# Two attention blocks on one core: a third score bank on loan by default, products with V gathered longer, and GpSimd held while VectorE makes a shift

## The chip, the core and the metric

The kernel runs on one core of a Trainium2 chip. The core has five engines that run their own queues in order and meet through semaphores: TensorE (PE, with PEld for its weight loads), VectorE (DVE), ScalarE (ACT), GpSimd (POOL) and SyncE (SP), which here only issues DMA transfers. The metric is the device time of one execution in microseconds, as the median of some runs; lower is better.

## The reference: what is computed

Two independent blocks with 2048 tokens, width 512 and 32 heads of 16 columns. Their outputs lie side by side in one 2048 x 1024 result. Block A is linear attention, block B is full softmax attention:

```
def _A_ref(x, wqkv, wo):      # q, k, v from x @ wqkv, 32 heads of 16
    phi = lambda t: jnp.where(t > 0, t + 1, jnp.exp(t)) + 1e-6
    pq, pk = phi(q), phi(k)
    kv = jnp.einsum("bhsd,bhse->bhde", pk, v)
    z = jnp.einsum("bhsd->bhd", pk)
    num = jnp.einsum("bhqd,bhde->bhqe", pq, kv)
    den = jnp.einsum("bhqd,bhd->bhq", pq, z)[..., None] + 1e-6
    o = num / den             # heads joined, @ wo
def _B_ref(x, wqkv, wo):
    scores = jnp.einsum("bhqd,bhkd->bhqk", q, k) * Dh ** -0.5
    p = _softmax(scores, axis=-1)
    o = jnp.einsum("bhqk,bhkd->bhqd", p, v)   # heads joined, @ wo
```

Nearly all the work is block B: 32 heads x 2048 x 2048 scores, each of which needs an exponential.

## The kernel before, in words

The scores are cut into 32 units (a group of eight heads, 512 query columns, one of two halves of the heads), and each unit into 64 blocks of 128 keys x 512 queries: 2048 blocks. A block's score product is one matmul from 32 rows of QT and KM into one PSUM bank (L863). Its exponential is made in one of two ways.

- **The exact way.** ScalarE takes the exponential of two or three neighbouring banks of pS in one instruction (L1095) and writes PT. There are two such slots, one of three banks and one of two (ABL), used in turn. A block then needs one product with V (L1224).
- **The approximate way**, called D here. VectorE turns one bank of scores into 16-bit integers whose bits are a half-precision number close to the exponential (L970, into DI, two banks at once where they lie side by side). Two shifted copies of it are needed as well (L1166, into DJ); a group of three blocks (DG) is shifted by one instruction of 1536 columns, twice. GpSimd makes most of these shifts, VectorE a few. A D block needs three products with V, one with each of DI and the two DJ, against three scaled copies of V (L671 makes the two scaled ones).

PSUM has eight banks: five for the slots, one for the sum of products with V (pPV), two for everything else (pD): D blocks, the projections of both blocks, block A. The third bank of the wide slot can be *lent* to that other work; the slot is then filled with two blocks instead of three (fill_act_cand, want_lend). Block A and the projections are jobs of a few stages each (Job) which the program threads between the blocks.

The order on every engine is not written by hand. A planner in the kernel's own Python code keeps a clock for each engine and a price for each operation, picks again and again the operation that can start first, and records it (Sched.add). From the recorded order it puts a semaphore wait wherever one engine reads or overwrites what another made. The engines then run their recorded queues in order. Constants near the top set the planner's habits: LD, LB and PB5 when the third bank is lent, VHI how many finished blocks may wait before products with V are preferred, PBL how much shift work may pile up, LATE how close to ScalarE's need a slot is filled, JU when a job may start ahead of its due time, SEEDS a random scatter of those due times by stages of 45 us.

In shift_cand (L1148) a shift goes to VectorE where GpSimd's pile is over LM = 5 us longer; its planned price there is 0.40 + w * 0.0003 us.

## Time and profile before

| what | us |
|---|---|
| median of 3 runs | 683.81 (683.69 to 686.09) |
| the profiled execution: its time | 684.12 |
| the profiled execution: span from first to last instruction | 682.4 |
| ScalarE busy | 669.0 (98%) |
| PE busy (matmul) | 653.9 (96%) |
| GpSimd busy | 622.1 (91%) |
| VectorE busy | 582.6 (85%) |
| granted TensorE clock, mean | 0.997 |

Busy time of an engine is the union of its instructions. Neighbouring instructions on ScalarE and VectorE overlap a little in the record, so the time that one more instruction costs is the distance between two starts, not the duration of one; both are used below. A PE that is busy in the record is not a PE at its peak.

### The profile page before, as it was taken

The numbers are of one execution on the slowest core, as the hardware profiler recorded it, in microseconds if no ns is written. First come the engines' busy times: TensorE is split into PE (matmuls) and PEld (weight loads), VectorE is DVE, ScalarE is ACT, GpSimd is POOL, SyncE is SP. The second block draws the span as 40 slices with busy tenths as digits, with TensorE's granted clock in tenths as the row PEclk, the third lists the DMA queues.
The fourth block names the chain that finished last, engine by engine and source line by source line (L and its number), as shares of the span: only waits on it lengthen the run. The fifth ranks groups of instructions, "written<-read, shape, count | busy, mean of one in ns | idle before, by whom it ended". The sixth has DMA issues, their size and how long they took to land.

```text
span 682.4 us, 19594 instructions
## 1 busy us (share of the span) xinstructions
PE 653.9 (96%) x8530; PEld 209.9 (31%) x8530; DVE 582.6 (85%) x937; ACT 669.0 (98%) x706; POOL 622.1 (91%) x470
## 2 busy tenths in 40 slices
PE   8999999999999999999999999999999999999997
PEld 4323333222323333332322233222332222322223
DVE  5878898999789988868999898888888998898983
ACT  5999999999999999999999999999999999999997
POOL 6698999999699999999999999999999999999894
PEclk9999999999999999999999998999999999999999
DMA  9400012011101201130111000111010110001111
GB/s 207 103 2 2 17 16 35 10 31 23 34 2 33 33 17 17 22 82 11 24 25 33 24 18 18 24 47 25 18 36 13 33 32 25 9 17 33 47 41 35
DMA packets 55418, 21.76 MB, mean 32 GB/s; under 512 B 45600, under 2 KB 55328, under 8 KB 55328
## 3 DMA queue, kind: packets, MB, share of 16 engines
q1 hardware_dynamic: 54128, 20.07, 13.4%
q8 instruction: 68, 1.11, 0.7%
q10 hardware_dynamic: 1200, 0.39, 0.2%
q14 instruction: 22, 0.18, 0.1%
HBM read 4.19 MB, written 4.19 MB: 12 GB/s over the span
## 4 chain that ended last, share of the span: by engine, by line
ACT 87%; POOL 7%; PE 3%; DVE 2%; DMA 1%; issue 0%; ACTq 0%
ACT PT L1095 85%; POOL DJ L1166 6%; ACT pD L683 1%; DVE DI L970 1%; PE pS L863 1%; DMA xTb<-in_B_x_dram 1%; ACT pS L683 1%; PE pD L535 1%; PE pPV L1224 1%; PE pS L535 1%; PE pS L654 0%; POOL XN L1359 0%; ACT KV L539 0%; POOL VV L671 0%; DVE DJ L1166 0%
## 5 line engine op out<-in xcount | busy, mean ns | idle before, releaser
L1095 ACT ACTIVATE PT<-pS 128x1024 f16<-128x1024 f32 (+1 forms) x666 | 660.5, 1353 | 2.6 <-PE pS L863 1.8
L1166 POOL TENSOR_SCALAR DJ<-DI 128x1536 int16<-128x1536 int16 (+1 forms) x391 | 579.5, 1483 | 48.0 <-DVE DI L970 21.6
L970 DVE TENSOR_SCALAR DI<-pD 128x512 uint16<-128x512 f32 (+1 forms) x456 | 315.2, 705 | 48.4 <-PE pD L863 42.8
L863 PE MATMUL pS<-QT,KM 32*128 32x512 bf16 x1573 | 261.5, 385 | 21.3 <-ACT PT L1095 15.0
L1224 PE MATMUL pPV<-PT,VV 128*17 128x512 f16 (+1 forms) x1420 | 244.0, 378 | 0.5 <-DVE OT L1354 0.5
L1224 PE MATMUL pPV<-DJ,VV 128*17 128x512 f16 (+1 forms) x1256 | 231.9, 379 | 0.7 <-POOL DJ L1166 0.5
L863 PE MATMUL pD<-QT,KM 32*128 32x512 bf16 x475 | 168.5, 385 | 0.3 <-DVE PQT L684 0.3
L863 PEld LDWEIGHTS pS<-QT,KM 32*128 32x128 bf16 x1573 | 64.3, 91 | 278.0 <-ACT PT L1095 260.3
L1224 PE MATMUL pPV<-DI,VV 128*17 128x512 f16 (+1 forms) x628 | 148.3, 379 | 0.5 <-DVE OT L1354 0.4
L970 DVE TENSOR_SCALAR DI<-pS 128x512 uint16<-128x512 f32 x153 | 104.1, 681 | 8.0 <-PE pS L863 4.4
L1224 PEld LDWEIGHTS pPV<-PT,VV 128*17 128x17 bf16 x1420 | 49.8, 88 | 44.0 <-issue 38.1
L1224 PEld LDWEIGHTS pPV<-DJ,VV 128*17 128x17 bf16 x1256 | 47.9, 88 | 47.2 <-issue 35.6
L863 PEld LDWEIGHTS pD<-QT,KM 32*128 32x128 bf16 x475 | 39.7, 91 | 9.3 <-issue 4.1
L1224 PEld LDWEIGHTS pPV<-DI,VV 128*17 128x17 bf16 x628 | 31.2, 88 | 22.4 <-issue 18.4
L1166 DVE TENSOR_SCALAR DJ<-DI 128x1536 int16<-128x1536 int16 x29 | 28.3, 977 | 0.0
L535 PE MATMUL pD<-xTb,Wb 128*32 128x512 bf16 (+1 forms) x368 | 26.7, 379 | 0.0
L535 PE MATMUL pD<-Wa,xTa 128*32 128x256 bf16 x672 | 26.4, 275 | 0.0
L1354 DVE STREAM_TRANSPOSE OT<-pPV 128x512 f32<-128x512 f32 x31 | 22.0, 708 | 0.7 <-PE pPV L1224 0.6
L1359 POOL TENSOR_TENSOR XN<-OT,ZRA 128x256 bf16<-128x256 f32 x31 | 19.5, 630 | 1.2
L683 ACT ACTIVATE pD<-pD 128x512 f32<-128x512 f32 x22 | 19.6, 893 | 0.0
L671 POOL TENSOR_SCALAR VV<-VV 128x544 bf16<-128x544 bf16 x24 | 17.3, 723 | 0.9
L535 PEld LDWEIGHTS pD<-Wa,xTa 128*32 128x32 bf16 x672 | 15.4, 96 | 8.7 <-issue 5.4
(109 smaller groups left out, 392.3 us busy)
## 6 DMA issues: line engine op xcount, KB each, us to landing
out_dram<-KV SPq DMA_DIRECT2D x31, 128.0 KB, 1.7
Wa<-in_A_wqkv_dram SPq DMA_DIRECT2D x3, 512.0 KB, 4.2
KM<-KR SPq DMA_DIRECT2D x96, 16.0 KB, 1.8
Wb<-in_B_wqkv_dram SPq DMA_DIRECT2D x2, 384.0 KB, 4.6
Wb<-in_B_wqkv_dram SPq DMA_DIRECT2D x1, 512.0 KB, 4.4
Wa<-in_A_wo_dram SPq DMA_DIRECT2D x1, 512.0 KB, 4.5
Wb<-in_B_wo_dram SPq DMA_DIRECT2D x1, 512.0 KB, 3.8
xTa<-in_A_x_dram SPq DMA_TRANSPOSE x24, 3.4
```

The lines of the kernel that those rows point to most:

```text
L535: ins = e.matmul(out[32 * g:32 * g + 32], lhsT=lhsT[:, 32 * g:32 * g + 32], rhs=rhs, start=start, stop=stop, tile_position=(0, 32 * g))
L671: st.append((lane, 0.74 if lane == "dve" else VVT, f_op(lane, lambda e, k=k: e.tensor_scalar(vv(k), vv(0), SW[k], 0.0, op0=ALU.mult, op1=A ...
L683: ex = lambda bk: sch.add("act", lambda e: e.activation(x(bk), x(bk), ACTF.Exp), reads=[bk[3]], writes=[bk[3]])
L863: return e.matmul(dst, lhsT=KM[32 * g:32 * g + 32, Gp % 2, e_, j * 128:(j + 1) * 128], rhs=QT[32 * g:32 * g + 32, Gp % 2, c * 512:(c + 1) ...
L970: sch.add("dve", lambda e: e.tensor_scalar(DI.bitcast(U16)[:, buf, i * 512:(i + n) * 512], f32v(DBANK[bi], 512 * n), EB, IMAX, op0=ALU.add ...
L1095: sch.add("act", lambda e: e.activation(PT[:, row, c0:c0 + w], SCR[sl][:, 0:w], ACTF.Exp, scale=SC / ESC), reads=skeys(sl)[:len(bl)], writ ...
L1166: sch.add(ln, lambda e: e.tensor_scalar(J, I, 1.0, float(SH[k]), op0=ALU.mult, op1=ALU.add), reads=[("DI", buf, i) for i in range(n)], wri ...
L1224: sch.add("pe", lambda e: e.matmul(dst[32 * g:32 * g + 17, 0:n], lhsT=VV[:, Gp % 2, k, j, 17 * h:17 * h + 17], rhs=P[:, q0:q0 + n], start= ...
L1354: sch.add("dve", lambda e: e.transpose(OT[:, 0, :], PVb[:, 0:512]), reads=[("PV", g) for g in range(4)], writes=[("OT", 0)])
L1359: mul = f_op("pool" if XNP else "dve", lambda e: e.tensor_tensor(xn[:, :, 16 * e_:16 * e_ + 16], o[:, :, 0:16], zr.unsqueeze(2).broadcast_ ...
```

## The change

What it does, part by part:

- **Lending.** want_lend now lends the third bank whenever no bank of pD is free at that time and VectorE's and GpSimd's piles are under LB = 2 and PB5 = 9 us (LD = 2), or when more banks are held by jobs than are lent. Before, it was lent while a job held a bank or waited for one.
- **Gathering.** The threshold VHI (24), and with it DLEAD, JU, LATE and PBL, become five sets, MODES; each stage of 45 us takes the set that its seed selects. The thresholds in the sets are 28, 36 or 48.
- **Holding.** When VectorE makes a shift, or a scaled copy of V, the next instruction recorded for GpSimd gets a wait for it (Sched.hold). The planner's price of such a shift on VectorE becomes 0.45 us after the end of GpSimd's running instruction.
- **The first products** (first_units) use the whole width of the array instead of four tiles of 32 columns, and the planner's starting clocks change, GpSimd's from 16.0 to 8.4.
- DG stays 3. SEEDS is new, so jobs are due at other times.

The core of the diff ("..." marks what is left out):

```
+        self.hold = []
...
+        if lane == "pool" and self.hold:
+            extra_deps = list(extra_deps) + self.hold
+            self.hold = []
...
-    PVW = 0.3
+    PVW = 0.0
-    LD = 1
-    LB = 99.0
-    PB5 = 3.0
+    LD = 2
+    LB = 2.0
+    PB5 = 9.0
-    PBL = 7.5
-    SEEDS = (0, 195, 365, 131, 7, 89, 76, 286, 0, 222, 34, 197, 397, 382, 371)
+    SEEDS = (0, 242, 225, 232, 372, 115, 142, 52, 152, 183, 352, 31, 0, 263, 361)
-    VHI = 24
+    MODES = ((0.8, 36, 0.7, 0.2, 9.0), (1.2, 36, 0.7, 0.2, 9.0), (0.8, 48, 0.9, 0.2, 10.5), (1.2, 28, 0.7, 0.1, 9.0), (1.0, 36, 0.55, 0.35, 8.0))
+    LDA = 1
+    JM = 0.8
+    DSH = 0.45
...
+        def mode():
+            return MODES[SEEDS[min(int(T["pe"] / SEG), len(SEEDS) - 1)] % len(MODES)]
...
-                        ins = mm4(e, bk[0][:, bk[2] + o0:bk[2] + o0 + n], Wb[:, cc, kind * 512:kind * 512 + 128], xTb[:, cc, c0:c0 + n], cc == 0, cc == 3)
+                        ins = e.matmul(bk[0][:, bk[2]:bk[2] + n], lhsT=Wb[:, cc, kind * 512:kind * 512 + 128], rhs=xTb[:, cc, c0:c0 + n], start=(cc == 0), stop=(cc == 3))
...
+                if lane == "dve":
+                    def alone(bk, cp=cp):
+                        sch.hold.append(cp(bk))
+                        sch.hold[-1].x = 0.27
+                    alone.kind = "x"
+                    st.append(("dve", 0.27, alone))
...
         def want_lend(t_):
...
+            free = sum(1 for x in dfree if x is not None and x <= t_ + 0.1)
+            if LD == 2 and sum(1 for i in range(len(dfree)) if held.get(i)) > sum(lent):
+                return True
+            if free:
                 return False
...
+            return d_backlog(t_) <= LB and p_backlog(t_) <= PB5
...
-            dp, dd = POOLT(w), 0.40 + w * 0.0003
+            dp, dd = POOLT(w), DSH + max(0.0, T["pool"] - sd)
...
+                if ln == "dve":
+                    T["pool"] = max(T["pool"], vis("dve", en_))
...
+                if ln == "dve":
+                    sch.hold.append(op)
+                    op.x = DSH
...
-            pr = 1 if out_ >= VHI or final else 4
+            pr = 1 if out_ >= mode()[1] or final else 4
...
-        T.update(pe=7.75, act=7.4, dve=9.05, pool=16.0)
+        T.update(pe=7.8, act=7.4, dve=9.2, pool=8.4)
```

Where the instructions stand now. Line numbers of the changed kernel are larger (L1095 becomes L1111, L1166 becomes L1184, L970 becomes L988, L535 becomes L544 and, for the first products, L573, L863 becomes L881, L654 becomes L664).

ScalarE, from its first exponential on; 1024 columns are two banks, 1536 are three. Before:

```order
L1095 ACTIVATE PT<-pS 128x1024 x14
L1095 ACTIVATE PT<-pS 128x1536
L1095 ACTIVATE PT<-pS 128x1024
L1095 ACTIVATE PT<-pS 128x1536
L1095 ACTIVATE PT<-pS 128x1024
L1095 ACTIVATE PT<-pS 128x1536
L1095 ACTIVATE PT<-pS 128x1024
L1095 ACTIVATE PT<-pS 128x1536
```

And in the change:

```order
L1111 ACTIVATE PT<-pS 128x1024 x6
L1111 ACTIVATE PT<-pS 128x1536
L1111 ACTIVATE PT<-pS 128x1024 x13
L1111 ACTIVATE PT<-pS 128x1536
L1111 ACTIVATE PT<-pS 128x1024 x3
L1111 ACTIVATE PT<-pS 128x1536
L1111 ACTIVATE PT<-pS 128x1024 x15
L1111 ACTIVATE PT<-pS 128x1536
```

Three-bank exponentials come one at a time between long rows of two-bank ones; over the program they go from 86 to 65 and the two-bank ones from 579 to 604.

PE, its first products after the warm-up; before:

```order
L535 MATMUL pS<-xTb,Wb 32x128 x16
L535 MATMUL pD<-xTb,Wb 32x256 x32
L535 MATMUL pS<-xTb,Wb 32x384 x16
L863 MATMUL pS<-QT,KM 128x512 x2
L535 MATMUL pD<-xTb,Wb 32x512 x16
L863 MATMUL pS<-QT,KM 128x512 x5
```

And in the change:

```order
L573 MATMUL pS<-xTb,Wb 128x128 x4
L573 MATMUL pD<-xTb,Wb 128x256 x8
L573 MATMUL pS<-xTb,Wb 128x384 x4
L544 MATMUL pD<-xTb,Wb 32x512 x8
L881 MATMUL pS<-QT,KM 128x512 x2
L881 MATMUL pD<-QT,KM 128x512
```

The 64 narrow products become 16 wide ones, and half of the next projection (8 tiles of L544) now stands ahead of the first scores.

VectorE, near the end of the program: the last rows of the last unit but one, up to the transpose (L1354, then L1374) that closes it. Before:

```order
L539 CAST KV<-pD 128x512
L970 TENSOR_SCALAR DI<-pD 128x512 x2
L970 TENSOR_SCALAR DI<-pS 128x512
L970 TENSOR_SCALAR DI<-pD 128x512 x2
L970 TENSOR_SCALAR DI<-pS 128x512
L539 CAST KV<-pD 128x512
L970 TENSOR_SCALAR DI<-pD 128x512
L1354 STREAM_TRANSPOSE OT<-pPV 128x512
```

And in the change:

```order
L988 TENSOR_SCALAR DI<-pD 128x512
L1184 TENSOR_SCALAR DJ<-DI 128x1536
L548 CAST KV<-pD 128x512
L1184 TENSOR_SCALAR DJ<-DI 128x1536
L548 CAST KV<-pD 128x512
L988 TENSOR_SCALAR DI<-pD 128x512
L988 TENSOR_SCALAR DI<-pS 128x512
L988 TENSOR_SCALAR DI<-pD 128x512 x2
L1374 STREAM_TRANSPOSE OT<-pPV 128x512
```

Shifts (DJ<-DI) now stand in VectorE's queue between the evictions; there are 64 of them in the program instead of 29, and GpSimd has 364 of three blocks instead of 389.

More of the change, by code (lines that the diff above doesn't have):

```diff
@@ L19 @@
     __slots__ = ("idx", "lane", "fn", "pos", "waits", "sig", "count", "vc",
-                 "name", "queue")
+                 "name", "queue", "x")
 class Sched:
@@ L53, in add @@
         op.sig = force_signal
+        op.x = None
         op.count = 0
@@ L1049, in fill_act_cand @@
             start = max(T["pe"], t0, afree[sl], ptfree.get((row, sl), 0.0) - 0.5)
-            if sl == 0 and wd == ABL[0] and lent[0]:
-                start = max(start, dfree[ND])
+            if sl in LIX and wd == 3 and lent[sl]:
+                start = max(start, dfree[LIX[sl]])
             dur = switch("q") + 0.22
-            late = T["act"] + sum(exps) - dur - TAIL["pe"] - SEM - LATE
+            late = T["act"] + sum(exps) - dur - TAIL["pe"] - SEM - mode()[3]
             if nfill[0] >= NS and start < late:
@@ L1061, in run @@
                 nfill[0] += 1
-                if sl == 0 and wd == ABL[0]:
-                    dfree[ND] = None
-                    lent[0] = False
-                elif sl == 0 and not lent[0]:
-                    dfree[ND] = st
-                    lent[0] = True
+                if sl in LIX and wd == 3:
+                    dfree[LIX[sl]] = None
+                    lent[sl] = False
+                elif sl in LIX and not lent[sl]:
+                    dfree[LIX[sl]] = st
+                    lent[sl] = True
                 afree[sl] = None
@@ L1317, in ahead_cand @@
         def ahead_cand():
-            assert cur_unit() is not None or not lent[0]
             if cur_unit() is not None or not ahead:
@@ L1437, in job_cand @@
             best = None
-            bi = min((i for i in range(ND + 1) if dfree[i] is not None), key=lambda i: dfree[i], default=None)
+            bi = min((i for i in range(len(dfree)) if dfree[i] is not None), key=lambda i: dfree[i], default=None)
             for lst, pr in ((urgent, 0.5), (early, 2), (bjobs, 2.2), (urgent2, 2.3), (ajobs, 2.5), (late, 2.7)):
```

79 lines of the change are left out of this document (38 added, 41 removed).

## The prediction

> **What bounds the kernel now.** I read the page's head first, with the chain of work that ended last, then the timeline of ScalarE at both ends, then one steady stretch of the windows.
>
> ```profile
> span 682.4 us, 19594 instructions
> ACT 87%; POOL 7%; PE 3%; DVE 2%; DMA 1%; issue 0%; ACTq 0%
> 10.41 30.68 ACT L1095 ACTIVATE PT<-pS 128x1024 f16<-128x1024 f32 x31 [0.56 <-PE pS L863]
> 674.48 1.51 ACT L1016 ACTIVATE PT<-pS 128x768 f16<-128x768 f32 x2
> 425.00:510.00 85.00, 81.75 (x1026) 24.70 (x1026) 72.96 (x118) 85.00 (x88) 81.21 (x60) 1.00 0.14 30
> ```
>
> ScalarE works without a break from 10.41 us to 675.99, and in the stretch from 425 to 510 it is busy 85.00 of 85.00 us. The columns there are PE, PEld, DVE, ACT, POOL: GpSimd with 81.21 is the next fullest, VectorE has 12 us to spare. The 7% of GpSimd in the chain lie in one place:
>
> ```profile
> 347.11 1.47 POOL DJ L1166
> 348.66 1.47 POOL DJ L1166
> 350.22 1.47 POOL DJ L1166
> POOL DJ L1166 <- DVE DI L970: 21.6, 16, 5.0
> PEld pS L863 <- ACT PT L1095: 260.3, 588, 1.4
> DVE DI L970 <- PE pD L863: 46.1, 99, 2.0
> ```
>
> The first three rows are from the chain of waits in order of time: shifts start every 1.55 us, back to back. The other three are from the list of waits (total us, times, longest). GpSimd waits 21.6 us for work in all, 5.0 of it before its first shift, so about 16.6 us of slack lie in the 660 us between. PE waits before 588 fills, 260.3 us in all, 0.44 us each: it is early, and its 96% busy is no bound. So the end is set by ScalarE, with GpSimd close behind, and what the change does to these two decides.
>
> **ScalarE's work.** The groups by shape, a run of ten two-bank exponentials, and two rows of PE's timeline at the end (the last fill and the last products with V):
>
> ```profile
> L1095 ACT ACTIVATE PT<-pS 128x1024 f16<-128x1024 f32 x579 | 574.9, 1299 | 2.6 <-PE pS L863 1.8 <-PE pD L863 0.8
> L1095 ACT ACTIVATE PT<-pS 128x1536 f16<-128x1536 f32 x86 | 148.2, 1723 | 0.0
> 594.96 9.18 ACT PT L1095 x10
> 674.04 0.10 PEld L863 LDWEIGHTS pS<-QT,KM 32*128 32x128 bf16 x3 [0.54 <-ACT PT L1095]
> 676.04 0.09 PEld L1224 LDWEIGHTS pD<-PT,VV 128*17 128x17 bf16 x3 [0.16 <-ACT PT L1016]
> ```
>
> Two banks cost 9.18 / 10 = 0.918 us from start to start. A third bank adds 1723 - 1299 = 424 ns, so three cost 1.342 us, one 0.494. By the order the change has 604 instead of 579 of two banks (+25 x 0.918 = +22.95 us), 65 instead of 86 of three (-21 x 1.342 = -28.18), and not the single one-bank instruction (-0.49): **-5.72 us**. The two closing pieces of 768 columns (1.51 us in the timeline above) become two of 256, another -0.85, which I don't count: after the last fill PE still has 12 projection tiles and 22 half products to make, and before it took from the fill at 674.04 to 676.04 with as much, so I let PE set that moment. The gain is 16 blocks, 1420 to 1404 on ScalarE and 628 to 644 on the D way. The price of more instructions for fewer blocks (671 for 668) is in these sums.
>
> **The shift on VectorE and the hold.** One case, with GpSimd's and VectorE's rows:
>
> ```profile
> 63.93 1.47 POOL L1166 TENSOR_SCALAR DJ<-DI 128x1536 int16<-128x1536 int16 x1
> 65.48 1.66 POOL L1166 TENSOR_SCALAR DJ<-DI 128x1536 int16<-128x1536 int16 x1
> 64.91 0.90 DVE L1166 TENSOR_SCALAR DJ<-DI 128x1536 int16<-128x1536 int16 x1
> 65.73 0.67 DVE L970 TENSOR_SCALAR DI<-pD 128x512 uint16<-128x512 f32 x1
> 12.35 0.69 DVE L970 TENSOR_SCALAR DI<-pS 128x512 uint16<-128x512 f32 x1
> 12.95 0.69 DVE L970 TENSOR_SCALAR DI<-pD 128x512 uint16<-128x512 f32 x1
> 13.13 6.11 POOL L1166 TENSOR_SCALAR DJ<-DI 128x1536 int16<-128x1536 int16 x4 [5.03 <-DVE DI L970]
> ```
>
> GpSimd's first shift ends at 65.40 and VectorE's ends 0.41 us later, at 65.81: it seems to sit until GpSimd is through and then needs about 0.4. GpSimd's next shift starts 0.08 us after its last, inside VectorE's, and takes 1.66 instead of 1.47. With the hold that next shift starts after VectorE's end and a semaphore: the last DI of the first group ends at 12.35 + 0.69 = 13.04 and GpSimd starts at 13.13, so 0.09. GpSimd then stands 0.41 + 0.09 = 0.50 us instead of 0.08 (+0.42), without the stretched row (0.19 before). VectorE's cost is the same with or without the hold, 65.73 - 64.91 = 0.82.
>
> The Trainium skill, "SBUF — State Buffer", section "Who interferes with whom", says that a VectorE instruction using both ports and a GpSimd instruction exclude each other for the whole instruction, and the later one is fully blocked. This trace agrees within 0.1 us: blocked until 65.73, a 1.47 us shift would end at 67.20, and it ends at 67.14. By that rule the hold speaks against the change, since GpSimd was kept out anyway: the semaphore would cost 64 x (0.42 - 0.19) = 15 us of GpSimd's time, an estimate by the page, and buy only that the recorded order is kept. No run here has yet shown the hold.
>
> GpSimd's sum, with these group rows:
>
> ```profile
> L1166 POOL TENSOR_SCALAR DJ<-DI 128x1536 int16<-128x1536 int16 x389 | 578.2, 1488 | 47.8 <-DVE DI L970 21.6
> L1166 DVE TENSOR_SCALAR DJ<-DI 128x1536 int16<-128x1536 int16 x29 | 28.3, 977 | 0.0
> L1166 POOL TENSOR_SCALAR DJ<-DI 128x512 int16<-128x512 int16 x2 | 1.2, 618 | 0.2
> L671 DVE TENSOR_SCALAR VV<-VV 128x544 bf16<-128x544 bf16 x8 | 5.5, 706 | 0.1
> ```
>
> 25 shifts fewer are -25 x 1.55 = -38.8 us. Two shifts of one block become two of two blocks, halfway from 618 to 1488 ns, +0.9. The shifts on VectorE now cost 64 x 0.42 = 26.9 where 29 cost 29 x 0.19 = 5.5: +21.4. The 8 copies of V keep their number; at about half a hold each, +1.6. In all **-14.9 us**, against 5.7 that ScalarE gets shorter. GpSimd's slack grows from 16.6 to about 26 us. What waits behind a held GpSimd is its whole queue of shifts and, for their DJ, PE's products; eight DJ buffers lie between. If VectorE comes late to a shift, GpSimd stands idle for it: both ends of that unknown are 0 (it comes while GpSimd still works, as in the row above) and the lateness of VectorE's longest wait, 2.0 us, per hold. I take 0.1 us, near the row seen: 72 x 0.1 = 7 us, inside the slack.
>
> **VectorE's work.** From the groups:
>
> ```profile
> L970 DVE TENSOR_SCALAR DI<-pD 128x512 uint16<-128x512 f32 x437 | 292.1, 683 | 44.5 <-PE pD L863 38.9 <-PE pS L863 2.2
> L970 DVE TENSOR_SCALAR DI<-pD 128x1024 uint16<-128x1024 f32 x19 | 23.1, 1217 | 3.9 <-PE pD L863 3.9
> ```
>
> One bank costs 12.95 - 12.35 = 0.60 from start to start, so the overlap is 0.09 and a pair costs 1.217 - 0.09 = 1.13. The order shows 36 more single banks (+21.6), 10 fewer pairs (-11.3) and 35 more shifts at 0.82 (+28.7): **+39 us**, 582.6 to about 622 of 677, 92% instead of 85%. It hides in VectorE's own gaps, 46.1 us of which are waits for pD. If that cover goes, a bank comes free late, the next D block starts late, and after it PE and GpSimd.
>
> **PE.** 32 more products with V, counted whole: eight of them take about 0.6 us, so +2.4 us, hidden in the 260.3 us that PE waits before fills. Gathering longer changes the number of turns between scores and products with V by about 1% in the order, so I cost it at nothing, with two sides: at best fewer late fills, at worst ScalarE waits behind a long run of products. It also lets PT and DJ stay taken longer.
>
> **The start.** PE's first products and what follows:
>
> ```profile
> 5.97 0.61 PE L535 MATMUL pS<-xTb,Wb 128*32 128x128 bf16 x16 [0.36 <-DMA xTb<-in_B_x_dram]
> 6.37 1.45 PE L535 MATMUL pD<-xTb,Wb 128*32 128x256 bf16 x32
> 7.65 0.82 PE L535 MATMUL pS<-xTb,Wb 128*32 128x384 bf16 x16
> 8.39 0.09 PEld L863 LDWEIGHTS pS<-QT,KM 32*128 32x128 bf16 x2 [0.32 <-DVE QT L571]
> 8.72 1.05 PE L535 MATMUL pD<-xTb,Wb 128*32 128x512 bf16 x16
> 9.98 0.10 PEld L863 LDWEIGHTS pS<-QT,KM 32*128 32x128 bf16 x4 [0.20 <-DVE KM L568]
> L654 PE MATMUL pD<-Wb,xTb 128*128 128x128 bf16 x208 | 15.6, 220 | 0.0
> ```
>
> The tiles last from 5.97 to 8.47. Whole-width products of 128 columns take 15.6 / 208 = 0.075 us each; scaled by columns the sixteen come to 0.3 + 1.2 + 0.8 = 2.3 us, 0.2 less. Half a projection (1.05 / 2 = 0.53) then stands ahead of the first scores, while the second fill, which waited until 9.98, may come up to 0.5 earlier, which is the 0.56 that ScalarE idled there. Between -0.5 and +0.5; I take **-0.2**.
>
> **The sum.** 684.12 was the profiled execution's time, 1.7 above its span and 0.3 above the median 683.81; I work from the median. 683.81 - 5.72 - 0.2 = 677.9. ScalarE's own idle time before was 2.6 us, and two-bank cycles leave PE less room (0.918 us against 1.342), so I add 0.6: **678.5 us**, 0.8% less. A difference of under 0.5% (3.4 us) can hardly be told from no change.
>
> **Rivals.**
> - *Late fills eat the gain* (no change, 681.5). For it: PE was not early in some 80 of the 668 fills, narrow fills are more frequent, and VectorE at 92% frees pD banks later, on which the fills that bring D blocks along wait. It needs some 40 fills that are late by 0.1 us. Against it: 579 of the fills were narrow before, with 2.6 us of idle time in all.
> - *The held GpSimd becomes the bound* (slower). VectorE comes late to its shifts, and GpSimd's queue stands each time. It decides from 26 / 72 = 0.36 us a hold, where the slack is gone, and is slower than before from (26 + 6) / 72 = 0.44. At 0.55 us the time is 677.9 + 72 x 0.55 - 26 = 691.5. For it: VectorE's waits for pD go up to 2.0 us. Against it: where GpSimd is in the chain it runs back to back, so it is behind VectorE there, and a hold on a VectorE that is ahead has passed by then.
> - *The third bank isn't lent in effect.* The order shows lent D blocks, DI from pS, only from 153 to 177, and three-bank exponentials from 86 to 65: the step from "often" to "nearly always" is small. The gain is then that of the 16 blocks, which is what the sum holds, so this is inside the forecast.
> - *The new order also removes old losses* (675): the back-to-back stretch of GpSimd from 347 on, with ScalarE's idle time, goes away: 677.9 - 2.6 = 675.3. It belongs to the forecast's low side.
>
> **Chances.** Forecast, the low side with it: 0.67. Late fills: 0.19. GpSimd bound: 0.14. So faster 0.67, same 0.19, slower 0.14. The forecast's own range is 674.5 to 680.4: the low end is the 675.3 with another 0.5 from the start and 0.3 of the uncounted 0.85. The late fills run on to 687.2. The range 674.5 to 687 leaves out most of the slower case and little below.
>
> **What would show it.** In the changed profile: ScalarE busy about 663 us and still without gaps after the first fills (a gap of over 3 us in all speaks for late fills); 604 and 65 exponentials at 0.918 and 1.342; VectorE busy about 622; shifts on VectorE with about 0.9 us each; GpSimd's shifts after a hold back at 1.47 instead of 1.66, with 0.5 us before them; its waits for VectorE's shifts under 36 us in all beyond that. If GpSimd's rows name DVE DJ with more than 0.8 us a time, and ScalarE shows gaps, the second rival was right. The forecast is also wrong if the tail after the last exponential, 6.4 us before (675.99 to 682.4), grows by more than a microsecond, or if the granted clock falls.

## The result, and the profile after

The changed kernel takes 679.59 us in the median of 8 runs (678.43 to 681.53), the kernel before 683.97 in 8 runs beside them (683.38 to 686.09). The ratio is 0.993, with a 95% interval of 0.9915 to 0.9944. The profiled execution took 679.04 us, its span 677.3.

The head of the page of the changed kernel, with the chain of work that ended last, and the same stretch from 425 to 510 us (the columns are PE, PEld, DVE, ACT, POOL):

```profile
span 677.3 us, 19632 instructions
PE 644.5 (95%) x8514; PEld 206.5 (30%) x8514; DVE 597.9 (88%) x998; ACT 661.7 (98%) x709; POOL 579.4 (86%) x445
ACT 94%; PE 5%; DMA 1%; issue 0%; ACTq 0%
425.00:510.00 85.00, 81.84 (x1048) 23.14 (x1040) 78.97 (x129) 85.00 (x92) 72.44 (x54) 1.00 0.13 29
```

ScalarE is still busy for the whole of the stretch. What changed stands beside it: GpSimd fell from 81.21 to 72.44 of 85 us, VectorE rose from 72.96 to 78.97, and GpSimd's 7% of the chain are gone. Its groups and its waits (total us, times, longest):

```profile
L1111 ACT ACTIVATE PT<-pS 128x1024 f16<-128x1024 f32 x604 | 585.6, 1279 | 2.2 <-PE pS L881 1.6 <-PE pD L881 0.7
L1111 ACT ACTIVATE PT<-pS 128x1536 f16<-128x1536 f32 x65 | 109.9, 1691 | 0.0
L1184 DVE TENSOR_SCALAR DJ<-DI 128x1536 int16<-128x1536 int16 x64 | 41.4, 650 | 0.0
L1184 POOL TENSOR_SCALAR DJ<-DI 128x1536 int16<-128x1536 int16 x364 | 536.4, 1474 | 78.8 <-DVE DJ L1184 44.9 <-DVE DI L988 8.5 <-DVE VV L681 3.1
...
PEld pS L881 <- ACT PT L1111: 243.2, 545, 0.9
DVE DI L988 <- PE pD L881: 30.5, 86, 1.3
POOL DJ L1184 <- DVE DI L988: 8.5, 7, 4.1
POOL DJ L1184 <- DVE DJ L1184: 44.9, 54, 1.9
```

ScalarE idles 2.2 us before its exponentials, no more than before. A shift on VectorE takes 650 ns on average, where the 29 of the kernel before took 977. GpSimd stands 44.9 us for VectorE's shifts, 0.83 us each, and only 8.5 us for lack of work, 4.1 of these before its first shift.

Two rows of ScalarE's timeline, the first exponentials and the last:

```profile
9.07 4.79 ACT L1111 ACTIVATE PT<-pS 128x1024 f16<-128x1024 f32 x5 [1.57 <-PE pS L881]
...
666.87 0.97 ACT L1031 ACTIVATE PT<-pS 128x256 f16<-128x256 f32 x2
```

In the kernel before, the first ones stood so:

```profile
8.83 1.02 ACT L1095 ACTIVATE PT<-pS 128x1024 f16<-128x1024 f32 x1 [1.00 <-PE pS L863]
10.41 2.86 ACT L1095 ACTIVATE PT<-pS 128x1024 f16<-128x1024 f32 x3 [0.56 <-PE pS L863]
```

The last exponential ends at 667.84 instead of 675.99, **8.15 us earlier**. From there to the end of the span it takes 9.46 us instead of 6.41, **3.05 more**. The difference, 5.10, is that of the spans, 682.4 - 677.3.

### The profile page after: what moved, and what is told of

Its sections match the earlier page's. It is cut to its first block, busy times and chain, and to the rows that moved or that the text cites. A ratio compares the mean times of both kernels' runs of the same rounds, so it can differ in the third digit from the quotient of the medians.

```text
span 677.3 us, 19632 instructions
## 1 busy us (share of the span) xinstructions
PE 644.5 (95%) x8514; PEld 206.5 (30%) x8514; DVE 597.9 (88%) x998; ACT 661.7 (98%) x709; POOL 579.4 (86%) x445
## 4 chain that ended last, share of the span: by engine, by line
ACT 94%; PE 5%; DMA 1%; issue 0%; ACTq 0%
ACT PT L1111 91%; PE pS L881 1%; ACT pD L701 1%; PE pPV L1245 1%; ACT pS L701 1%; DMA xTb<-in_B_x_dram 1%; PE pS L544 1%; PE pD L544 1%; PE pD L1245 0%; PE pD L664 0%; PE pS L573 0%; PE pD L573 0%; ACT KV L548 0%; ACTq L1606 0%; ACTq L1333 0%
## 5 line engine op out<-in xcount | busy, mean ns | idle before, releaser
L1111 ACT ACTIVATE PT<-pS 128x1024 f16<-128x1024 f32 (+1 forms) x669 | 651.5, 1319 | 2.2 <-PE pS L881 1.6
L1184 POOL TENSOR_SCALAR DJ<-DI 128x1536 int16<-128x1536 int16 x366 | 538.5, 1471 | 79.0 <-DVE DJ L1184 44.9
L988 DVE TENSOR_SCALAR DI<-pD 128x512 uint16<-128x512 f32 (+1 forms) x458 | 310.6, 693 | 35.3 <-PE pD L881 27.7
L881 PE MATMUL pS<-QT,KM 32*128 32x512 bf16 x1581 | 262.1, 384 | 23.1 <-ACT PT L1111 16.6
L1245 PE MATMUL pPV<-PT,VV 128*17 128x512 f16 (+1 forms) x1404 | 231.5, 378 | 0.0
L1245 PE MATMUL pPV<-DJ,VV 128*17 128x512 f16 (+1 forms) x1288 | 222.4, 378 | 0.0
L881 PE MATMUL pD<-QT,KM 32*128 32x512 bf16 x467 | 166.6, 384 | 0.0
L881 PEld LDWEIGHTS pS<-QT,KM 32*128 32x128 bf16 x1581 | 65.1, 90 | 282.6 <-ACT PT L1111 243.2
L988 DVE TENSOR_SCALAR DI<-pS 128x512 uint16<-128x512 f32 x177 | 120.5, 681 | 6.8 <-PE pS L881 2.9
L1184 DVE TENSOR_SCALAR DJ<-DI 128x1536 int16<-128x1536 int16 x64 | 41.4, 650 | 0.0
L881 PEld LDWEIGHTS pD<-QT,KM 32*128 32x128 bf16 x467 | 39.3, 91 | 6.5 <-issue 3.2
L544 PE MATMUL pD<-xTb,Wb 128*32 128x512 bf16 x400 | 30.5, 383 | 0.0
L544 PE MATMUL pD<-Wa,xTa 128*32 128x256 bf16 x672 | 25.6, 274 | 0.0
L1374 DVE STREAM_TRANSPOSE OT<-pPV 128x512 f32<-128x512 f32 x31 | 22.0, 709 | 1.5 <-PE pPV L1245 1.2
L544 PEld LDWEIGHTS pD<-Wa,xTa 128*32 128x32 bf16 x672 | 15.2, 96 | 8.8 <-issue 6.3
L701 ACT ACTIVATE pD<-pD 128x512 f32<-128x512 f32 x19 | 15.7, 827 | 0.0
```

The source lines that it names most:

```text
L544: ins = e.matmul(out[32 * g:32 * g + 32], lhsT=lhsT[:, 32 * g:32 * g + 32], rhs=rhs, start=start, stop=stop, tile_position=(0, 32 * g))
L701: ex = lambda bk: sch.add("act", lambda e: e.activation(x(bk), x(bk), ACTF.Exp), reads=[bk[3]], writes=[bk[3]])
L881: return e.matmul(dst, lhsT=KM[32 * g:32 * g + 32, Gp % 2, e_, j * 128:(j + 1) * 128], rhs=QT[32 * g:32 * g + 32, Gp % 2, c * 512:(c + 1) ...
L988: sch.add("dve", lambda e: e.tensor_scalar(DI.bitcast(U16)[:, buf, i * 512:(i + n) * 512], f32v(DBANK[bi], 512 * n), EB, IMAX, op0=ALU.add ...
L1111: sch.add("act", lambda e: e.activation(PT[:, row, c0:c0 + w], SCR[sl][:, 0:w], ACTF.Exp, scale=SC / ESC), reads=skeys(sl)[:len(bl)], writ ...
L1184: op = sch.add(ln, lambda e: e.tensor_scalar(J, I, 1.0, float(SH[k]), op0=ALU.mult, op1=ALU.add), reads=[("DI", buf, i) for i in range(n)] ...
```

## The experiments

Of each kernel the *count* is given: two-bank exponentials x 0.918 + three-bank ones x 1.342 us (0.494 for a one-bank one), with the prediction's prices. It is 647.4 us before and 641.7 in the change. What a kernel takes beside its count is called the *rest*. So that runs of different hours can stand together, a time in the table at the end is the measured ratio times 684.0.

**The hold taken away, everything else in place.** Every engine keeps the order of the change.

```
                 if ln == "dve":
-                    sch.hold.append(op)
-                    op.x = DSH
```

(and the same for the copies of V).

> The changed kernel with GpSimd's wait for VectorE's shifts left out; prices, plan and order on every engine stay those of the change. Theory A (time follows ScalarE's work, the hold lies off the path): 679.6 us within 1; GpSimd's 45 us of waits for DVE DJ are gone, VectorE's shift goes from 650 ns back to about 900 and VectorE's busy time from 598 to about 612. Theory B (the hold itself brings the gain, by keeping VectorE's shifts short and the engines in the planned order): at least 682, with ScalarE's gaps growing.

Measured: 689.02 us (12 runs), ratio to the kernel before 1.0049 (1.0031 to 1.0067). Without its semaphore the change loses all its gain and more, about 8 us. The group of the shift, two waits and the chain of this kernel:

```profile
L1183 DVE TENSOR_SCALAR DJ<-DI 128x1536 int16<-128x1536 int16 x64 | 59.9, 940 | 0.0
...
PEld pS L880 <- DVE DI L987: 13.1, 26, 0.9
PEld pD L880 <- DVE DI L987: 8.1, 22, 1.0
...
ACT 75%; PE 12%; DVE 10%; DMA 1%; issue 1%; ACTq 0%
```

The same two waits in the change:

```profile
PEld pS L881 <- DVE DI L988: 9.9, 19, 0.9
PEld pD L881 <- DVE DI L988: 2.6, 8, 0.4
```

The same 64 shifts cost 940 ns instead of 650, PE waits 21.2 us instead of 12.5 for VectorE ahead of these fills, and VectorE is in the chain with 10%. From the first exponential to the last it is 6.6 us longer than in the change (665.39 against 658.77, by the two traces), and ScalarE's stops in between grow from 0.65 to 5.2 us. The same shift in both kernels shows why; first in the change, VectorE's and GpSimd's timelines:

```profile
44.84 0.55 DVE L1184 TENSOR_SCALAR DJ<-DI 128x1536 int16<-128x1536 int16 x1
45.48 1.47 POOL L1184 TENSOR_SCALAR DJ<-DI 128x1536 int16<-128x1536 int16 x1 [0.81 <-DVE DJ L1184]
```

And without the hold (this profile runs 2.1 us later, from the first exponential on, at 11.14 instead of 9.07; see the start below, which is no effect of the hold):

```profile
46.65 1.47 POOL L1183 TENSOR_SCALAR DJ<-DI 128x1536 int16<-128x1536 int16 x1
46.91 1.62 DVE L1183 TENSOR_SCALAR DJ<-DI 128x1536 int16<-128x1536 int16 x1
```

Here GpSimd's next shift is under way when VectorE comes, 0.26 us later. VectorE's ends at 48.53, 0.41 after GpSimd's end at 48.12. In the change GpSimd stands from 44.67 to 45.48 and VectorE's shift, alone, takes 0.55. Over the program, 49 of the 64 shifts begin without the hold while GpSimd is at work, and these take 1.06 us on average; in the change it is 30, at 0.77 us. The hold so decides who goes first: it shifts the waiting from VectorE, which has evictions queued behind its shift and frees PE's banks with them, to GpSimd, which has slack.

The later start is one of the single execution. The second group of first products, in the change and then without the hold:

```profile
6.48 1.04 PE L573 MATMUL pD<-xTb,Wb 128*128 128x256 bf16 x8
```

```profile
7.12 1.92 PE L573 MATMUL pD<-xTb,Wb 128*128 128x256 bf16 x8
```

They took 1.92 us in the run with the later hint below too, whose order is that of the change, hold included, and whose first exponential came at 11.28. So of the 8.6 us between the spans of these two profiles some 2 don't belong to the hold. In the medians, where early and late starts mix, the difference is about 8, in the part between the exponentials 6.6.

**The hold alone, in the kernel before.** The same wait after VectorE's 29 shifts; nothing in the plan knows of it.

```
+        if lane == "pool" and self.hold:
+            extra_deps = list(extra_deps) + self.hold
+            self.hold = []
...
+                if ln == "dve":
+                    sch.hold.append(op)
```

> The kernel before with nothing but the wait of GpSimd for VectorE's 29 shifts; order as before. Theory A: GpSimd, back to back there, loses 29 x 0.23 us and some lateness, 7 to 15 us of its 16.6 us of slack; the time is 684 to 687, not faster. Theory B: VectorE's shifts get shorter (977 to about 700 ns) and the time falls to 682 or less.

Measured: 685.90 us (12 runs), ratio 1.0018 (1.0001 to 1.0036). It gains nothing. Its group and its chain:

```profile
L1170 DVE TENSOR_SCALAR DJ<-DI 128x1536 int16<-128x1536 int16 x29 | 31.4, 1082 | 0.0
ACT 69%; POOL 13%; PE 11%; DVE 4%; issue 1%; DMA 1%; DVEq 0%; ACTq 0%
```

The shift isn't even shorter, since the old plan places it where GpSimd still has a shift to finish that was recorded earlier, which no wait keeps back (27 of the 29 begin while GpSimd is at work); and GpSimd, which had less slack there, gets a larger part of the chain. The hold pays in an order in which GpSimd has run out its earlier work by then, which the new price (from the end of GpSimd's running instruction) is made to bring about; no run has the hold with the old price in a plan of its own, so this is argued.

**The end of the program.** All engines wait for ScalarE's last copy before the flag and the branch, so that no engine leaves while stores are still being issued.

```
+                e.wait_ge(sems["act"], totals["act"])
                 e.wait_ge(sems["dve"], flag_op.count)
```

> The changed kernel, but at the program's end every engine waits for ScalarE's last copy before it reads the flag and branches. Theory C (the last two stores land late, 4.1 instead of 1.7 us, because the instruction fetch after the early branch takes their DMA engines): stores land in about 1.8 us again, the tail from the last exponential falls from 9.5 to about 7.5 us and the time by about 2 us, to 677.5. Theory D (the stores are slow by themselves, or the fetch must be paid anyway): 679.6 or up to 1 us more.

Measured: 679.27 us (6 runs), ratio 0.9936 (0.9911 to 0.9961): the time of the change. The stores from SP's queue (KB each, us to landing), in the kernel before, in the last 18 us of its span:

```profile
out_dram<-KV SPq DMA_DIRECT2D x3, 128.0 KB, 1.7
```

in the change, in its last 5 us, with the fetches of instructions in the same stretch:

```profile
q14 instruction: 4, 0.03, 2.9%
q8 instruction: 1, 0.02, 2.4%
out_dram<-KV SPq DMA_DIRECT2D x2, 128.0 KB, 4.0
```

and in this experiment, from 671.5 to 674.5 us, where no instruction is fetched:

```profile
out_dram<-KV SPq DMA_DIRECT2D x2, 128.0 KB, 1.7
```

So the two last stores take 4.0 us where they run beside the fetches and 1.7 where they don't. But it saves nothing: the fetches then come after the stores (3 and 1 in the last 2.9 us), and the span ends at 677.4 instead of 677.3. The wait moves from the stores to VectorE: its last instruction comes 3.35 us behind its branch, where it is 0.55 in the kernel before and 2.9 in the change.

**The branch's code hinted later.** The program gives PE, ScalarE and VectorE a hint of the coming branch, 60 recorded operations before the end of each queue; here VectorE gets it 24 before.

```
-                           mark=(HINT, lambda e: loc.append(e.mark_branch_hint_location())) if queue in HQ else None)
+                           mark=(24 if queue == "dve" else HINT, lambda e: loc.append(e.mark_branch_hint_location())) if queue in HQ else None)
```

> The changed kernel with VectorE's branch prefetch hint 24 instead of 60 recorded operations before its end; nothing else. The run with the late branch showed the stores landing in 1.7 us again but VectorE standing 3.4 us between its branch and its last drain (0.55 in the kernel before), with an instruction fetch in that time. Theory C2 (VectorE's branch target is fetched after the branch, since what the hint fetched is gone by then, and that fetch also holds up the last stores in the changed kernel): VectorE's drain comes within 1 us of its branch, the stores land in about 1.8 us, the tail falls from 9.5 to 7.3 us, the time by about 2 us to 677.5. Rival (the place of the hint doesn't matter): 679.6.

Measured: 679.81 us (6 runs), ratio 0.9926 (0.9908 to 0.9944), the last stores took 3.8 us, and VectorE's last instruction came 3.0 us behind its branch: no effect. What is fetched there in spite of the hint stays open.

**The old rule of lending in the changed kernel, planned anew.**

```
-    LD = 2
-    LB = 2.0
-    PB5 = 9.0
+    LD = 1
+    LB = 99.0
+    PB5 = 3.0
```

(with the body of want_lend as it was before).

> The changed kernel with the old lending rule (lend while a job holds a bank or waits for one); the plan is made anew. Its order has 680 two-bank and 11 three-bank exponentials and 654 D blocks: 639.0 us of ScalarE's work by 0.918 and 1.342, where the change has 641.7. VectorE makes 96 shifts instead of 64. Theory A: 2.7 us faster, about 677. Rival (VectorE, 32 x 0.57 us = 18 us fuller, frees banks late and ScalarE waits): 679.6 or more, with gaps on ScalarE over 4 us.

Measured: 685.50 us (12 runs), ratio 1.001 (0.999 to 1.0029), with a count of 639.0, lower than the change's. Its page and its waits:

```profile
PE 651.3 (95%) x8539; PEld 203.9 (30%) x8539; DVE 620.7 (91%) x1025; ACT 660.3 (97%) x731; POOL 545.4 (80%) x423
POOL DJ L1184 <- DVE DJ L1184: 73.2, 66, 5.2
L1111 ACT ACTIVATE PT<-pS 128x1024 f16<-128x1024 f32 x680 | 638.0, 1226 | 8.6 <-PE pD L881 4.7 <-PE pS L881 3.7
```

In this plan the old rule sends more, not fewer, blocks to VectorE (96 shifts on it, 91% busy), GpSimd stands up to 5.2 us at a time, and ScalarE waits 8.6 us before its two-bank exponentials. The count falls by 2.7 and the rest grows by 8.

**The change without hold and with the old price, planned anew.** 30 shifts on VectorE, count 647.6.

```
-            dp, dd = POOLT(w), DSH + max(0.0, T["pool"] - sd)
+            dp, dd = POOLT(w), 0.40 + w * 0.0003
```

(and no hold, and a shift on VectorE no longer moves the planner's clock of GpSimd.)

> The changed kernel without the hold and with the old planned price of a shift on VectorE (0.40 + w * 0.0003), planned anew: an order that expects what VectorE does without a hold. It has 528 two-bank and 121 three-bank exponentials (647.6 us, where the change has 641.7 and the kernel before 647.4) and 30 shifts on VectorE. If ScalarE's work decides where VectorE isn't over-planned: 679.6 + 5.9 = 685.5, like the kernel before, and its shifts on VectorE take about 0.95 us. If the hold and its price bring nothing by themselves: 680 or less.

Measured: 695.84 us (4 runs), ratio 1.0169 (1.0147 to 1.019), 10 us more than expected by the count. Its shift costs 1020 ns, ScalarE idles 7.8 us before its exponentials, and 4.23 us instead of 2.81 ahead of its first final copy. The kernel before has the same price and no hold either. Of the 11.8 us between the spans of the two profiles, 6.1 are stops of ScalarE between its exponentials (7.7 against 1.6) and 4.0 the tail behind the last one; why this order has them isn't separated here.

**Products with V gathered no longer than before.** All five sets of MODES with 24.

```
-    MODES = ((0.8, 36, 0.7, 0.2, 9.0), (1.2, 36, 0.7, 0.2, 9.0), (0.8, 48, 0.9, 0.2, 10.5), (1.2, 28, 0.7, 0.1, 9.0), (1.0, 36, 0.55, 0.35, 8.0))
+    MODES = ((0.8, 24, 0.7, 0.2, 9.0), (1.2, 24, 0.7, 0.2, 9.0), (0.8, 24, 0.9, 0.2, 10.5), (1.2, 24, 0.7, 0.1, 9.0), (1.0, 24, 0.55, 0.35, 8.0))
```

> The changed kernel with the threshold of waiting blocks at the old 24 in all five sets, planned anew: 527 two-bank and 126 three-bank exponentials, 652.9 us of ScalarE's work, 11.2 more than the change; 46 shifts on VectorE. If ScalarE's work decides: 679.6 + 11.2 = 690.8. If gathering is only about PE's turns and the order would have held without it: 680 to 684.

Measured: 692.80 us (4 runs), ratio 1.0125 (1.0104 to 1.0146). ScalarE idles 3.1 us before its exponentials, against 2.2 in the change; in the main it has more to do (count 652.9, 46 shifts on VectorE of 627 ns).

**No shift on VectorE at all.**

```
-    LM = 5.0
+    LM = 99.0
```

> The changed kernel where a shift never goes to VectorE (its limit at 99 us), planned anew: 534 two-bank and 121 three-bank exponentials, 652.6 us, 10.9 more than the change, and 410 shifts on GpSimd. If ScalarE's work decides: about 690.5, with ScalarE as gapless as in the change. If VectorE's 64 shifts are what costs time: under 680.

Measured: 701.18 us in a single run. GpSimd's share and, from the timelines, ScalarE's longest stop and what GpSimd did ahead of it:

```profile
PE 656.8 (94%) x8485; PEld 214.1 (31%) x8485; DVE 555.1 (79%) x907; ACT 673.6 (96%) x695; POOL 646.1 (92%) x491
386.12 2.37 ACT L1111 ACTIVATE PT<-pS 128x1024 f16<-128x1024 f32 x2 [4.59 <-PE pS L881]
369.80 10.73 POOL L1184 TENSOR_SCALAR DJ<-DI 128x1536 int16<-128x1536 int16 x7
```

GpSimd is at 92%, with at least seven shifts back to back ahead of that stop, and ScalarE waits 4.59 us for a fill; its stops between exponentials come to 9.5 us, so the first theory (as gapless as the change) fails as well as the second. That 410 shifts are more than GpSimd carries is not shown: the chain of this run has ScalarE with 89% and PE with 9%, GpSimd isn't in it, and ahead of that stop it names products of PE (with V, and 15 of a projection).

**Other scatters, the control for all that was planned anew.** The last four kernels have other orders, while SEEDS had been chosen for another plan. So the rules of the change with two other scatters (the sets of MODES by stage as they are):

```
-    SEEDS = (0, 242, 225, 232, 372, 115, 142, 52, 152, 183, 352, 31, 0, 263, 361)
+    SEEDS = (35, 277, 260, 267, 407, 150, 177, 87, 187, 218, 387, 66, 35, 298, 396)
```

> The changed kernel with 35 added to every number of SEEDS: each stage of 45 us keeps its set of MODES (35 is a multiple of the five sets), only the random scatter of the jobs' due times differs. The new order has 541 two-bank and 112 three-bank exponentials, 647.4 us of ScalarE by the prices of the prediction against 641.7 in the change, 626 D blocks against 644, and 44 shifts on VectorE against 64. Theory (the rules of the change carry its gain): 647.4 + 37.9 (what lies beside the count in the change: 679.6 - 641.7) = 685.3 us, and the shift on VectorE stays near 0.65 us, since the hold is in it. Rival (the gain is that of a scatter fitted to these rules, and an order with another scatter has late fills too, as the two replanned orders had): 690 to 697 us, with ScalarE gaps of 10 us or more beside the first fills and the end.

> The same with 100 added to every number: 537 two-bank and 112 three-bank exponentials, 643.8 us by count, 634 D blocks, 45 shifts on VectorE. Theory by count: 643.8 + 37.9 = 681.7 us. Rival (late fills come with any scatter that was not fitted): 687 to 693 us. If this run and the last differ by the 3.6 us of their counts, the count carries; if they differ otherwise, the losses beside the count are a matter of the single order.

and the kernel before with the scatter of the change:

```
-    SEEDS = (0, 195, 365, 131, 7, 89, 76, 286, 0, 222, 34, 197, 397, 382, 371)
+    SEEDS = (0, 242, 225, 232, 372, 115, 142, 52, 152, 183, 352, 31, 0, 263, 361)
```

> The kernel before with the SEEDS of the change and nothing else: 487 two-bank, 158 three-bank and one one-bank exponential, 659.6 us by count against 647.4 before, 596 D blocks against 628, 15 shifts on VectorE against 29. Theory (count): 659.6 + 36.4 (684.0 - 647.4 before) = 696.0 us. Rival (the scatter of before was fitted as well, and losses beside the count come on top): 700 us or more. Either way the kernel before loses by a foreign scatter about as much as the change does, and a replanned variant with the old numbers cannot be read below some 10 us.

Measured, three runs each: 687.81 us (ratio 1.0044, 1.0008 to 1.0081), 684.66 (0.9995, 0.9965 to 1.0025) and 698.92 (1.0211, 1.0166 to 1.0256). The first two differ by their counts, 3.6 us, within half a microsecond, though each ratio is known only within 0.3 to 0.4%, which is over 2 us. Both lie 2 to 3 us above the theory by count and below the rival's range. The shift on VectorE, of the first, then of the second, then of the third:

```profile
L1184 DVE TENSOR_SCALAR DJ<-DI 128x1536 int16<-128x1536 int16 x44 | 28.4, 646 | 0.0
```

```profile
L1184 DVE TENSOR_SCALAR DJ<-DI 128x1536 int16<-128x1536 int16 x45 | 29.1, 648 | 0.0
```

```profile
L1166 DVE TENSOR_SCALAR DJ<-DI 128x1536 int16<-128x1536 int16 x15 | 14.7, 980 | 0.0
ACT 95%; PE 2%; DMA 1%; SPq 1%; DVE 0%; issue 0%; ACTq 0%
```

The short shift goes with the rules, not with one order. And GpSimd's 7% of the chain before went with one order: the kernel before with another scatter has ScalarE alone in its chain, and is 14 us slower, because it does more exponentials in the exact way (count 659.6).

**Late numbers of SEEDS replaced.** This was meant to give a scatter with a lower count.

```
-    SEEDS = (0, 242, 225, 232, 372, 115, 142, 52, 152, 183, 352, 31, 0, 263, 361)
+    SEEDS = (0, 242, 225, 232, 372, 115, 142, 52, 152, 183, 352, 226, 0, 263, 281)
```

> The changed kernel with three numbers of SEEDS replaced (those of the stages from 495, 585 and 630 us on), the sets of MODES as they were; the order is the same up to about 495 us. It has 605 two-bank and 63 three-bank exponentials, 639.9 us by count against 641.7. Theory (the count carries the time where the rest of the order is kept): 639.9 + 37.9 = 677.8 us, ratio to the kernel before 0.991, 1.8 us under the change. Rival (the loss beside the count lies between 37.9 and 40.9 us in the orders with these rules, so a new scatter gives back more than the count saves): 679.5 to 681 us. Here a shorter run of PE stands between the last products with V and the end than in the change (36 projection tiles instead of 44 in its longest piece), which is for the theory.

(Two numbers differ, not three: those of the stages from 495 and from 630 us on.) Measured: 681.21 us (10 runs), ratio 0.995 (0.9935 to 0.9966). Its exponentials:

```profile
L1111 ACT ACTIVATE PT<-pS 128x1024 f16<-128x1024 f32 x595 | 579.0, 1278 | 4.4 <-PE pS L881 2.8 <-PE pD L881 1.6
L1111 ACT ACTIVATE PT<-pS 128x1536 f16<-128x1536 f32 x72 | 120.7, 1677 | 0.0
```

The groups show 595 and 72 exponentials, which count 642.8 us: the 605, 63 and 639.9 of the expectation were those of another order, so the premise of both theories was wrong. By its own count the theory gives 642.8 + 37.9 = 680.7, and 681.21 was measured. No order with a lower count than the change's was run with these rules, and none of the kernels beats the change by more than the measurement can tell.

All together:

| kernel | ratio to before | count, us | time, us | rest, us |
|---|---|---|---|---|
| before | 1 | 647.4 | 684.0 | 36.6 |
| the change | 0.993 | 641.7 | 679.2 | 37.5 |
| hold in the kernel before | 1.0018 | 647.4 | 685.2 | 37.8 |
| all wait before the branch | 0.9936 | 641.7 | 679.6 | 37.9 |
| hint at 24 | 0.9926 | 641.7 | 678.9 | 37.2 |
| kernel before, new scatter | 1.0211 | 659.6 | 698.4 | 38.8 |
| second scatter | 1.0044 | 647.4 | 687.0 | 39.6 |
| third scatter | 0.9995 | 643.8 | 683.7 | 39.9 |
| scatter changed late | 0.995 | 642.8 | 680.6 | 37.8 |
| gathering at 24 | 1.0125 | 652.9 | 692.6 | 39.7 |
| no hold | 1.0049 | 641.7 | 687.4 | 45.7 |
| old lending | 1.001 | 639.0 | 684.7 | 45.7 |
| no hold, old price | 1.0169 | 647.6 | 695.6 | 48.0 |
| no shift on VectorE (one run) | 1.0251 | 652.6 | 701.2 | 48.6 |

The rest is a reading aid, not a law: it holds the start, the projections' share of ScalarE and the end, and every wait. It is 36.6 to 39.9 us in ten of the kernels, and 45.7 to 48.6 in the four others (VectorE's shifts too long, twice; too many of them; or none). That GpSimd or VectorE is what lags there was shown for the run without hold alone.

## Why the prediction was right, and where it was not

Forecast 678.5, measured 679.59, inside the stated range: the forecast was right. That the sum came out so near is luck, because two errors offset each other. To the last exponential it had 5.9 us of gain and 0.6 of loss, and 8.15 were measured; behind it it had nothing, and 3.05 were lost. Of the signs that it set, ScalarE's 663 us and the counts came (661.7); VectorE's 622 us, its shifts of 0.9 us and the unchanged tail did not.

**ScalarE's work: right.** 604 and 65 exponentials, hardly a gap (2.2 us in all, 1.57 of them ahead of the first one), as the count had it. From the first to the last exponential it became 8.39 us shorter (8.15, and a first one that came at 9.07 instead of 8.83), and the sum's 5.72 is the main part. The starts in the two traces give the others. Stops of ScalarE between exponentials fell from 1.64 to 0.65 us, 0.99 less, 0.56 of which is the second fill. The two closing pieces took 0.97 instead of 1.51 us, 0.54 less, where the prediction had 0.85. The single one-bank exponential had cost 0.88 us and not 0.494, 0.39 more of a gain. And 0.7 lie in the spacing of all others, as two-bank ones follow each other in 916 instead of 918 ns. So the low side's case, *the new order also removes old losses*, was true for about 1 us, and GpSimd's 7% of the chain went with it. That this share belonged to the old order and not to the old rules, the kernel before with the new scatter shows; but ScalarE's stops are 2.6 us there, so that fewer of them come with the rules is not shown.

**The start: right in sum.** The first exponential came 0.24 later and the 0.56 at the second fill went away, so the start gave 0.32 us, where the prediction took 0.2. Its parts were off: the sixteen wide products took 1.92 us (6.24 to 8.16) instead of the 2.50 of the narrow ones, 0.58 less and not 0.2, and they began later, at 6.24 instead of 5.97, when the input had landed. Single executions differ by more than this: in the run with the late branch, whose start is the same program, the first exponential came at 8.88, in the run with the later hint at 11.28. The row of PE's timeline:

```profile
6.24 0.40 PE L573 MATMUL pS<-xTb,Wb 128*128 128x128 bf16 x4 [0.79 <-DMA xTb<-in_B_x_dram]
```

**The shift on VectorE: the step that failed.** The prediction said "VectorE's cost is the same with or without the hold, 0.82". The runs show 940 ns without it, 650 with it, in one and the same order, and 646 to 648 in two other orders. The 35 more shifts therefore cost (650 - 80) x 64 - (977 - 80) x 29 ns = 10.5 us instead of 28.7, with the 80 to 90 ns by which neighbours overlap. VectorE rose by 15.3 us instead of 39: counted from start to start in the two traces, 10.6 of them are the shifts, 7.1 the DI instructions, where the prediction had 10.3, and the others took 2.4 less. In the one case that the prediction had read, VectorE came 0.98 us into GpSimd's shift (64.91 against 63.93) and was kept some 0.5 us; in the one shown above it came after 0.26 us and was kept for 1.2. The Trainium skill, "SBUF — State Buffer", section "Who interferes with whom", has the one that comes later fully blocked, and both rows agree: VectorE's shift ends 0.41 us after GpSimd's in both. The rule was right, and the conclusion that a semaphore buys only the recorded order was not: the order is what decides which of the two is blocked.

**"It hides in VectorE's own gaps": wrong without the hold.** The prediction let VectorE reach 622 us at no cost. Without the hold it reaches 612.6, and is in the chain with 10%, at 8 us more. What hides isn't told by the share of busy time: an eviction behind a shift that takes 1.62 us can free its bank a microsecond late, where fills follow each other in 0.92.

**GpSimd: the price wrong, the verdict right.** It waits 44.9 us ahead of its shifts for those of VectorE, and 5.8 for VectorE's copies of V or ahead of other work, 50.7 in all, where the prediction had some 36 (64 x 0.42 + 1.6 + 7). Its busy time fell by 42.7, so in sum it has 8 us less room, where the prediction had 8 more (14.9 less the 7 of lateness). Its slack by the prediction's measure, the waits for DI behind the first shift, fell from 16.6 to 4.4 us (8.5 - 4.1), and about 26 were forecast. The 0.36 us a hold from which *the held GpSimd* should have become the bound was lateness, on top of the 0.50 that a hold was reckoned at; 0.83 a time is 0.33 on top. So that point was nearly reached and not passed: GpSimd isn't in the chain, and the gaps on ScalarE that the row set for that rival asked for as well didn't come. A GpSimd that is held catches up on work that it would otherwise have waited for, and the fall of its waits for DI fits that. By this measure little room is left for more holds.

**Late fills: wrong for this order.** ScalarE idled 2.2 us, and the 0.6 us added for it wasn't spent. With other scatters it was 4.0 and 3.7 (3.2 and 2.2 behind the first exponential, where the change has 0.65), so the price is real, and depends on the order.

**The end: "I let PE set that moment" was right, and not enough.** The prediction itself named a tail that grows by more than a microsecond as a failure. It grew by 3.05: a run of 44 projection products on PE keeps ScalarE idle for 2.81 us instead of 2.17 (0.64 more); its three final copies then take 2.20 us instead of 1.58 (0.62 more), the second of them waiting 0.52; and from the last copy to the end it is 4.45 instead of 2.66 us (1.79 more), where stores and fetches of instructions meet. What the rows of this stretch say, from the chain of waits and ScalarE's timeline of the change, and from ScalarE's timeline before:

```profile
668.17 2.46 PE pS L544 x44
...
670.65 0.60 ACT L548 ACTIVATE KV<-pS 128x512 bf16<-128x512 f32 x1 [2.81 <-PE pS L544]
671.77 0.60 ACT L548 ACTIVATE KV<-pD 128x512 bf16<-128x512 f32 x1 [0.52 <-PE pS L544]
672.26 0.59 ACT L548 ACTIVATE KV<-pS 128x512 bf16<-128x512 f32 x1
```

```profile
678.16 0.60 ACT L539 ACTIVATE KV<-pD 128x512 bf16<-128x512 f32 x1 [2.17 <-PE pD L535]
678.66 1.08 ACT L539 ACTIVATE KV<-pS 128x512 bf16<-128x512 f32 x2
```

In both kernels the span ends 0.5 us after the last store has landed (681.87 before, 676.79 in the change), so the 1.79 are stores that take longer. The experiment at the end gave the stores their 1.7 us back and no time; that the fetch is the cause of both waits is likely and not shown. In the kernel before, the last fetches lie in the last 0.9 us of the span, behind the stores:

```profile
q14 instruction: 3, 0.02, 8.7%
q8 instruction: 1, 0.02, 8.7%
```

There they cost nothing that the span shows. Why VectorE's last instruction follows its branch by 3.35 us in the experiment, where the fetches come behind the stores too, and by 0.55 in the kernel before, isn't settled.

**Gathering longer, "I cost it at nothing".** Its effect is in the count, so the sum held it unseen: with 24 in all sets the order does 11.2 us more on ScalarE and takes 13.4 more. Against the two other scatters, which are the fairer comparison, it is 5.6 to 8.9 us.

**Lending, and what can't be told.** The old rule in the new plan costs 5.5 us against the change, but 2.3 less to 1.0 more than the new rule with the other scatters. Its larger rest and VectorE at 91% are measured; that the new rule is the better one is not. The same holds for the kernel without hold and with the old price: part of its 16 us is a scatter made for another plan. The gain of 0.7% is that of one chosen order over another chosen order; with a scatter chosen for neither, the new rules were 11 to 15 us ahead of the old (687.0 and 683.7 against 698.4), from one such order of the old. The planner's other new constants (PVW, JM, its prices for PE) were in all runs with the new rules, and what they do isn't separated either.

## What to carry to other kernels

Where two engines keep each other out, ask which of them has work waiting behind it, and let that one go first with a semaphore on the other: here it made the same instruction 0.29 us shorter 64 times on average, and some 7 to 8 us of 680 hung on it; in an order not made for it the same semaphore gained nothing. Before a replanned variant is read as the effect of its rule, replan the unchanged rule with another random number: here that alone moved the time by 4 to 14 us. And when a long middle part gets shorter, look at what is done behind it, since a loss there isn't seen in the balance of the engines.

## What was not expected of the hardware

- A shift of 1536 columns on VectorE takes 0.55 us alone and 1.62 where GpSimd's is under way for 0.26 us already; GpSimd's restarts 0.09 us after VectorE's end (44.84 + 0.55 to 45.48). In the traces of the kernel before, of the hold alone and of the change without hold, 105 shifts on VectorE begin while GpSimd is at work, and 93 of them end 0.41 to 0.42 us after GpSimd's instruction.
- Two stores of 128 KB took 4.0 us to land beside fetches of instructions of 0.05 MB in all, and 1.7 without them.
- A hint of the branch to VectorE 24 or 60 operations ahead made no difference to these fetches (4 and 1 of them beside the stores in both).
- With the same order at the start, the first exponential came at 9.07 us in one execution and at 11.28 in another, as the first products took nearly twice as long (eight of 256 columns 1.04 and 1.92 us); the granted clock in the profile's rows is 1.00 in both.
